# Two column tiles of 64 in place of four of 32 for the projections behind the product with V

## The chip, the cores and the metric

The kernel runs on one core of a Trainium2 chip. The metric is device time in microseconds (us). A core has five engines with queues of their own: TensorE (PE, with its weight loads listed apart as PEld), VectorE (DVE), ScalarE (ACT), GpSimd (POOL) and SyncE (SP), which issues most DMAs here.

## The reference

Two independent problems A and B are computed and their outputs laid side by side. Each is an attention block with 32 heads of 32 channels, 2048 positions, 1024 channels and a window of 256 keys:

```
qkv = (x @ wqkv) -> q, k, v          # x: 2048 x 1024, wqkv: 1024 x 3072
scores = q @ k.T * 32 ** -0.5        # kept where 0 <= query - key < 256
o = softmax(scores) @ v              # by head
out = o @ wo                         # wo: 1024 x 1024
```

All inputs and outputs are bfloat16.

## The kernel before

Four heads make a group (4 x 32 = 128 partitions), so there are 16 groups over both problems. TensorE has three kinds of work, and each uses the 128 x 128 array in a form of its own:

- The scores (line 537) multiply 32 rows (the channels of one head) by 64 columns (keys). Four heads and two halves of the keys lie in the array at the same time. The form is written 32*64 in the trace.
- The product with V and the row sums of the softmax (line 618) use all 128 rows (keys) and 32 columns (the channels of one head), four heads side by side: 128*32. This is `pv`, and there are 128 of them, one for each group and pair of query blocks.
- The projections (q and k, V, and the output) use all 128 rows. They all go through the helper `by_columns`. While `whole[0]` is true it issues one multiplication of 128 columns (line 193, 128*128). Otherwise it issues the same work as four multiplications of 32 columns each, at the column positions 0, 32, 64 and 96 (line 197, 128*32). Each multiplication has a weight load of its own.

The program is written out by a planner in steps; 152 of them hold scores. A step issues the scores (`session`), then those products with V that are due, then as much projection work as the planner has put there, in chains of eight multiplications over the 1024 input channels. Two ScalarE instructions per step take the exponential (line 547). Products are due in every second step, and `whole[0]` is set to false in exactly these:

```
        whole[0] = not (due and due[0][0] <= now)
        session(now)
        while due and due[0][0] <= now:
            ...
            pv(pg, pk)
```

So TensorE goes through scores, products and projections of 32 columns in a step with products, and through scores and projections of 128 columns in one without. After the last product of all, `whole[0]` is true again, and the rest of the output projection is issued whole.

The planner counts one projection multiplication of 512 elements at `NS_MM` = 216 ns in either form (`clock.pe += NS_MM`), so the form has no part in the order. The result of a chain is copied out of PSUM by ScalarE or VectorE (`evacuate`), whichever the planner's clock finds earlier.

Of the kernel before, what the change touches and what calls it, by code (L numbers as in the profile page):

```python
# [18 lines left out]
P = 128  # L19
# [64 lines left out]
def _fast_path(ctx, tc, cfg, problems, outs, consts, certify, osbp, ps_acc, ps_proj, last_stores):  # L84
    nc = tc.nc
# [105 lines left out]
    def by_columns(out, lo, hi, lhsT, rhs, start, stop):  # L191
        if whole[0]:
            nc.tensor.matmul(out[:, lo:hi], lhsT=lhsT, rhs=rhs, start=start, stop=stop,  # L193
                             skip_group_check=True)
            return
        for c in range(0, P, 32):
            nc.tensor.matmul(out[c:c + 32, lo:hi], lhsT=lhsT[:, c:c + 32], rhs=rhs, start=start,  # L197
                             stop=stop, tile_position=(0, c), skip_group_check=True)

    side = []  # L200
# [23 lines left out]
    def qk_steps(g, which, k, lo=0, hi=512, st_=None, last=True):  # L224
        pi = g // T
        st_ = {} if st_ is None else st_
        steps = []
        for ct in range(CT):
            def f(ct=ct):
                if "pp" not in st_:  # L230
                    st_["pp"] = new_pp()
                by_columns(st_["pp"], lo, hi, wqk[g][:, ct, which, :], xT[(pi, k)][:, ct, lo:hi],
                           ct == 0, ct == CT - 1)
                clock.pe += NS_MM * (hi - lo) / 512.0
                if ct == CT - 1 and last:
                    dst = qk_tiles(g)[which][:, k * 512:(k + 1) * 512]
                    evacuate(dst, st_["pp"][:])
                    clock.ready[(g, which, k)] = clock.banks[-1]
            steps.append((NS_MM * (hi - lo) / 512.0, f))
        return steps  # L240

    def v_steps(m, b):
        pi = m // (T // VG)
        k, a = divmod(b, QB)
        st_ = {}
        steps = []
        w_ = VG * P
        for h in range(512 // w_):
            for ct in range(CT):
                def f(ct=ct, h=h):  # L250
                    if "pp" not in st_:
                        st_["pp"] = new_pp()
                        if (m, k) not in vts:
                            vts[(m, k)] = vp.tile([P, QB, w_], BF16, name="vt")
                    by_columns(st_["pp"], h * w_, (h + 1) * w_,
                               xT[(pi, k)][:, ct, (a + h) * P:(a + h + 1) * P],
                               wv[m][:, ct, :], ct == 0, ct == CT - 1)
                    clock.pe += NS_MM * w_ / 512.0
                    if ct == CT - 1 and h == 512 // w_ - 1:
                        evacuate(vts[(m, k)][:, a:a + h + 1, :],  # L260
                                 st_["pp"][:].rearrange("p (h w) -> p h w", w=w_))
                steps.append((NS_MM * w_ / 512.0, f))
        return steps
# [12 lines left out]
    def last_steps(pi, b, ch):  # L276
        k, a = divmod(b, QB)
        st_ = {}
        steps = []
        for lo in (0, 256):  # L280
            for ct in range(CT):
                def f(ct=ct, lo=lo):
                    if ct == 0:
                        st_["pp"] = ps_acc.tile([P, 512], F32, name="acc")
                    by_columns(st_["pp"], lo, lo + 256, oTs[(pi, k)][:, ct, a * P:(a + 1) * P],
                               wo_sb[(pi, ch)][:, ct, lo:lo + 256], ct == 0, ct == CT - 1)
                    clock.pe += NS_MM / 2
                    if ct == CT - 1:
                        store(pi, b, ch, lo, lo + 256, st_["pp"])
                steps.append((NS_MM / 2, f))  # L290
        return steps
# [684 lines left out]
```

## Time and profile before

| what | value |
|---|---|
| median of 3 runs | 598.64 us (598.45 to 598.72) |
| the profiled execution, its own time | 598.88 us |
| its span, from first to last instruction | 597.2 us |
| TensorE busy | 590.3 us (99%) |
| ScalarE busy | 405.6 us (68%) |
| GpSimd busy | 365.2 us (61%) |
| VectorE busy | 349.7 us (59%) |
| mean granted TensorE clock | 1.000 of full speed |

A multiplication is pipelined: the next one starts while the last is still running, and their ends are modelled. What a multiplication costs TensorE is therefore the distance from its start to the next start, not the mean duration in a row. The four multiplications of 32 columns of one group start within about 10 ns of each other and run side by side. In a merged row of the timeline, the start is that of the first instruction, and the length runs to the end of the last.

### The profile page before, as it was taken

The numbers are of one execution on the slowest core, as the hardware profiler recorded it, in microseconds if no ns is written. First come the engines' busy times: TensorE is split into PE (matmuls) and PEld (weight loads), VectorE is DVE, ScalarE is ACT, GpSimd is POOL, SyncE is SP. The second block draws the span as 40 slices with busy tenths as digits, with TensorE's granted clock in tenths as the row PEclk, the third lists the DMA queues.
The fourth block names the chain that finished last, engine by engine and source line by source line (L and its number), as shares of the span: only waits on it lengthen the run. The fifth ranks groups of instructions, "written<-read, shape, count | busy, mean of one in ns | idle before, by whom it ended". The sixth has DMA issues, their size and how long they took to land. (4 is left out here: it accounts for less than half of the span.)

```text
span 597.2 us, 31193 instructions
## 1 busy us (share of the span) xinstructions
PE 590.3 (99%) x13863; PEld 358.9 (60%) x13863; DVE 349.7 (59%) x969; ACT 405.6 (68%) x506; POOL 365.2 (61%) x918
## 2 busy tenths in 40 slices
PE   9999999999999999999999999999999999999997
PEld 6666666666656756566656657755556665555443
DVE  1265676567667677774566656665566557576100
ACT  4667777877787787766566766676768777774332
POOL 0558667877768787766466666666666667665000
PEclk9999999999999999999999999999999999999999
DMA  9915110111026102645111100113020040114222
GB/s 241 183 38 145 39 40 3 40 40 37 4 48 100 39 4 57 107 94 115 33 39 39 27 14 4 41 37 87 7 74 21 3 109 13 56 56 132 66 80 75
DMA packets 86813, 35.63 MB, mean 60 GB/s; under 512 B 65552, under 2 KB 86160, under 8 KB 86672
## 3 DMA queue, kind: packets, MB, share of 16 engines
q1 hardware_dynamic: 85344, 33.18, 23.1%
q8 instruction: 110, 1.80, 1.3%
q10 hardware_dynamic: 1328, 0.39, 0.3%
q14 instruction: 31, 0.25, 0.2%
HBM read 17.83 MB, written 8.39 MB: 44 GB/s over the span
## 5 line engine op out<-in xcount | busy, mean ns | idle before, releaser
L547 ACT ACTIVATE pt<-st 128x1024 bf16<-128x1024 f32 x304 | 300.0, 1025 | 74.5 <-PE st L537 35.9
L558 POOL TENSOR_SCALAR_AFFINE_SELECT diag<-pt 128x256 bf16<-128x256 bf16 x512 | 215.6, 446 | 181.9 <-ACT pt L547 175.8
L571 POOL TENSOR_SCALAR_AFFINE_SELECT pt<-pt 128x512 bf16<-128x512 bf16 (+1 forms) x256 | 155.4, 626 | 0.0
L585 DVE TENSOR_TENSOR both<-diag,pt 128x512 bf16<-128x512 bf16 (+1 forms) x256 | 124.3, 525 | 15.9 <-POOL diag L558 11.7
L197 PE MATMUL pp<-xT,wqk 128*32 128x512 bf16 x2120 | 125.1, 379 | 0.0
L193 PE MATMUL pp<-xT,wqk 128*128 128x512 bf16 (+1 forms) x542 | 121.5, 361 | 0.0
L193 PE MATMUL pp<-wv,xT 128*128 128x256 bf16 x920 | 109.3, 273 | 0.0
L628 DVE STREAM_TRANSPOSE turned<-acc 128x128 f32<-128x128 f32 x128 | 39.8, 311 | 106.2 <-PE acc L618 106.2
L193 PEld LDWEIGHTS <-xT 128*128 128x128 bf16 x920 | 89.2, 98 | 19.6
L197 PEld LDWEIGHTS <-wqk 128*32 128x32 bf16 x2120 | 54.0, 97 | 44.7
L193 PE MATMUL pp<-wo_sb,oT 128*128 128x512 bf16 x347 | 78.3, 379 | 0.2 <-DVE unsafe_i L917 0.2
L537 PEld LDWEIGHTS <-kT 32*64 32x64 bf16 x3904 | 41.0, 103 | 58.5 <-issue 58.5
L193 PEld LDWEIGHTS <-wqk 128*128 128x128 bf16 x542 | 46.5, 98 | 45.1 <-DMA wqk<-in_A_wqkv_dram 0.2
L537 PE MATMUL st<-qT,kT 32*64 32x64 bf16 (+4 forms) x3904 | 65.7, 236 | 0.8 <-issue 0.8
L635 DVE STREAM_TRANSPOSE wide<-inv 128x256 f32<-128x256 f32 x128 | 56.9, 445 | 4.2
L193 PEld LDWEIGHTS <-oT 128*128 128x128 bf16 x363 | 34.3, 98 | 38.4 <-issue 0.2
L216 ACT CAST osb<-pp 128x512 bf16<-128x512 f32 x48 | 28.1, 586 | 42.8 <-PE pp L193 29.3
L636 DVE TENSOR_TENSOR oT<-acc,wide 128x256 bf16<-128x256 f32 x128 | 54.3, 424 | 4.4
L618 PE MATMUL acc<-pt,vt 128*32 128x128 bf16 (+2 forms) x1792 | 48.8, 223 | 0.0
L618 PEld LDWEIGHTS <-vt 128*32 128x32 bf16 x2816 | 43.5, 97 | 7.7 <-issue 0.4
L216 ACT CAST vt<-pp 128x512 bf16<-128x512 f32 x45 | 26.5, 588 | 31.7 <-PE pp L193 27.4
L216 ACT CAST kT<-pp 128x512 bf16<-128x512 f32 x55 | 32.2, 585 | 17.5 <-PE pp L197 14.3
(49 smaller groups left out, 378.0 us busy)
## 6 DMA issues: line engine op xcount, KB each, us to landing
out_dram<-osb SPq DMA_DIRECT2D x63, 128.0 KB, 1.9
wqk<-in_B_wqkv_dram SPq DMA_DIRECT2D x32, 128.0 KB, 3.3
wqk<-in_A_wqkv_dram SPq DMA_DIRECT2D x24, 128.0 KB, 3.0
wo_sb<-in_A_wo_dram SPq DMA_DIRECT2D x16, 128.0 KB, 2.4
wv<-in_B_wqkv_dram SPq DMA_DIRECT2D x16, 128.0 KB, 3.0
wo_sb<-in_B_wo_dram SPq DMA_DIRECT2D x16, 128.0 KB, 2.3
oT<-in_A_x_dram SPq DMA_DIRECT2D x4, 256.0 KB, 5.1
wv<-in_A_wqkv_dram SPq DMA_DIRECT2D x2, 512.0 KB, 6.2
```

The lines of the kernel that those rows point to most:

```text
L193: nc.tensor.matmul(out[:, lo:hi], lhsT=lhsT, rhs=rhs, start=start, stop=stop, skip_group_check=True)
L197: nc.tensor.matmul(out[c:c + 32, lo:hi], lhsT=lhsT[:, c:c + 32], rhs=rhs, start=start, stop=stop, tile_position=(0, c), skip_group_check=True)
L216: nc.scalar.copy(out=out, in_=in_)
L537: nc.tensor.matmul(scores[c * HALF:(c + 1) * HALF, r, a * HALF:(a + w_) * HALF], lhsT=kT[rows, keys], rhs=qT[rows, q:q + w_ * HALF], start ...
L547: nc.scalar.activation(out=pt[:, lo:lo + 2, :n * HALF], in_=scores[:, lo:lo + 2, :n * HALF], func=ACT.Exp, bias=-SHIFT, scale=cfg.scale)
L558: nc.gpsimd.affine_select(out=diags[(g, p)][:, :, h, lo:lo + HALF], in_=pt[:, :, a * HALF:(a + 1) * HALF], pattern=[[0, 4], [1, HALF]], co ...
L571: nc.gpsimd.affine_select(out=blk, in_=blk, pattern=[[0, 4], [-1, w_ * HALF]], compare_op=ALU.is_gt, fill=0.0, base=-HALF * (us[a][2] - 3) ...
L585: nc.vector.tensor_tensor(out=both[:, :, h, o:o + w_], in0=dg[:, :, h, o:o + w_], in1=pts[t][:, :, a:a + w_], op=ALU.add)
L618: nc.tensor.matmul(acc[32 * r:32 * r + 32, o:o + w_], lhsT=lhsT, rhs=src[:, r, :], start=(x == 0), stop=(x == len(moves) - 1), tile_positi ...
L628: nc.vector.transpose(out=turned[:], in_=acc[:, 2 * P:3 * P])
L635: nc.vector.transpose(out=wide[:], in_=inv[:].unsqueeze(3).to_broadcast([P, 2, QB, 32]))
L636: nc.vector.tensor_tensor(out=oTs[(pi, k)][:, t, (p % 2) * 256:(p % 2 + 1) * 256], in0=acc[:, 0:256], in1=wide[:], op=ALU.mult)
```

## The change

The loop in `by_columns` steps over the 128 columns by 64, so the work that was four multiplications of 32 columns becomes two of 64 columns, at the column positions 0 and 64, with two weight loads in place of four. Which chains are issued in this form and when stays as it was.

```
-        for c in range(0, P, 32):
-            nc.tensor.matmul(out[c:c + 32, lo:hi], lhsT=lhsT[:, c:c + 32], rhs=rhs, start=start,
+        for c in range(0, P, 64):
+            nc.tensor.matmul(out[c:c + 64, lo:hi], lhsT=lhsT[:, c:c + 64], rhs=rhs, start=start,
                              stop=stop, tile_position=(0, c), skip_group_check=True)
```

The instructions of TensorE at the first of these stretches, before, at its beginning (the last row sum with `ones`, then the first projection) and at its end (the last projection, then the first scores of the next step); the size behind a multiplication is its output, columns of the array by elements:

```order
L618 LDWEIGHTS ones_58
L618 MATMUL acc_605<-both_512,ones_58 32x128
L197 LDWEIGHTS wqk_123
L197 MATMUL pp_657<-xT_137,wqk_123 32x512
...
L197 LDWEIGHTS wqk_134
L197 MATMUL pp_697<-xT_122,wqk_134 32x512
L537 LDWEIGHTS kT_254
L537 MATMUL st_296<-qT_253,kT_254 64x256
```

The same two places of TensorE's order in the changed kernel:

```order
L618 LDWEIGHTS ones_58
L618 MATMUL acc_605<-both_512,ones_58 32x128
L197 LDWEIGHTS wqk_123
L197 MATMUL pp_657<-xT_137,wqk_123 64x512
...
L197 LDWEIGHTS wqk_134
L197 MATMUL pp_681<-xT_122,wqk_134 64x512
L537 LDWEIGHTS kT_254
L537 MATMUL st_296<-qT_253,kT_254 64x256
```

Before, the array's form was the same (128 rows, 32 columns) on both sides of the beginning; now the columns go from 32 to 64 there. At the end the rows go from 128 to 32 in both kernels, and the columns from 32 to 64 before, from 64 to 64 now. Between the two places the 64 multiplications before are 32 now. Nothing else moves on any engine: over the whole executed order, line 197 follows line 618 at 76 places, line 537 follows line 197 at 74, and line 618 follows line 197 at 2.

## Rows read from the trace of the kernel before

**Rows 1.** The page: busy time of TensorE; its granted clock in 40 slices.
```profile
PE 590.3 (99%) x13863; PEld 358.9 (60%) x13863; DVE 349.7 (59%) x969; ACT 405.6 (68%) x506; POOL 365.2 (61%) x918
...
PEclk9999999999999999999999999999999999999999
```

**Rows 2.** Waits of TensorE: waiting engine and line <- releaser: total us, times, longest.
```profile
PE pp L676 <- DVE ones L895: 1.3, 1, 1.3
PE pp L197 <- issue: 1.0, 1, 1.0
PE st L537 <- issue: 0.8, 1, 0.8
PE pp L193 <- DVE unsafe_i L917: 0.2, 1, 0.2
```

**Rows 3.** Longest waits of all engines, same columns.
```profile
POOL diag L558 <- ACT pt L547: 175.8, 130, 14.4
DVE turned L628 <- PE acc L618: 106.2, 66, 4.0
```

**Rows 4.** Groups by line and shape: xcount | busy us, mean ns | idle before.
```profile
L197 PE MATMUL pp<-xT,wqk 128*32 128x512 bf16 x2120 | 125.1, 379 | 0.0
L618 PE MATMUL acc<-both,ones 128*32 128x128 bf16 x896 | 31.9, 219 | 0.0
L197 PE MATMUL pp<-wo_sb,oT 128*32 128x512 bf16 x628 | 37.0, 379 | 0.0
L197 PE MATMUL pp<-wv,xT 128*32 128x256 bf16 x416 | 12.9, 273 | 1.0 <-issue 1.0
L197 PEld LDWEIGHTS <-wqk 128*32 128x32 bf16 x2120 | 54.0, 97 | 44.7
L537 PEld LDWEIGHTS <-kT 32*64 32x64 bf16 x3904 | 41.0, 103 | 58.5 <-issue 58.5
```

**Rows 5.** Timeline of TensorE, two steps: start us, length us, what, xcount.
```profile
131.99 0.28 PE L618 MATMUL acc<-both,ones 128*32 128x128 bf16 x8
132.10 2.33 PE L197 MATMUL pp<-xT,wqk 128*32 128x512 bf16 x40
134.37 0.42 PE L537 MATMUL st<-qT,kT 32*64 32x128 bf16 x24
134.72 1.47 PE L193 MATMUL pp<-xT,wqk 128*128 128x512 bf16 x6
136.03 1.91 PE L193 MATMUL pp<-wv,xT 128*128 128x256 bf16 x16
137.87 0.42 PE L537 MATMUL st<-qT,kT 32*64 32x256 bf16 x20
```

**Rows 6.** Timeline of TensorE at 134.36 us: last projection group, first scores.
```profile
134.04 0.39 PE L197 MATMUL pp<-xT,wqk 128*32 128x512 bf16 x4
134.37 0.24 PE L537 MATMUL st<-qT,kT 32*64 32x128 bf16 x2
```

**Rows 7.** Timeline of TensorE at 137.86 us: last whole projection, first scores.
```profile
137.66 0.27 PE L193 MATMUL pp<-wv,xT 128*128 128x256 bf16 x1
137.87 0.34 PE L537 MATMUL st<-qT,kT 32*64 32x256 bf16 x8
```

**Rows 8.** Timeline of TensorE, 554.8 to 555.7 us: last product, then whole projections.
```profile
554.84 0.28 PE L618 MATMUL acc<-both,ones 128*32 128x128 bf16 x8
555.05 0.82 PE L193 MATMUL pp<-wo_sb,oT 128*128 128x512 bf16 x3
```

**Rows 9.** Timeline of TensorE at 546.3 us: whole projections, then a product.
```profile
545.83 0.59 PE L193 MATMUL pp<-wo_sb,oT 128*128 128x512 bf16 x2
546.35 0.24 PE L618 MATMUL acc<-pt,vt 128*32 128x64 bf16 x7
```

**Rows 10.** Timeline of TensorE at 550.4 us: projections of 32 columns, then a product.
```profile
549.95 0.60 PE L197 MATMUL pp<-wo_sb,oT 128*32 128x512 bf16 x8
550.38 0.23 PE L618 MATMUL acc<-pt,vt 128*32 128x128 bf16 x4
```

**Rows 11.** Timeline of TensorE: the first and the last of 76 passages from products to projections.
```profile
30.10 0.29 PE L618 MATMUL acc<-both,ones 128*32 128x128 bf16 x8
30.21 0.39 PE L197 MATMUL pp<-xT,wqk 128*32 128x512 bf16 x4
...
550.83 0.28 PE L618 MATMUL acc<-both,ones 128*32 128x128 bf16 x8
550.94 0.39 PE L197 MATMUL pp<-wo_sb,oT 128*32 128x512 bf16 x4
```

## The prediction, made before the changed kernel ran

> **What bounds the kernel now.** I read the page first, then the waits, then the timeline of TensorE. On the page the reader is to see that TensorE is busy for 590.3 of 597.2 us and that the granted clock stands at full speed in all 40 slices [rows 1], so that no change of clock is in play. Busy time alone doesn't prove a bound, since multiplications overlap; the waits do. All of TensorE's waits come to 3.3 us, of which only 0.2 us lies after the start-up and is for another engine; two holes of 1.0 and 0.8 us have no releaser at all [rows 2]. The others wait for TensorE or for what follows it: VectorE alone waits 106.2 us for the products with V [rows 3]. So what TensorE loses or gains is lost or gained in the end, nearly one for one, and the question is how far apart its multiplications start.
>
> **Inside a run of projections nothing is to be had.** The stretch from 132.10 us holds 40 multiplications of 32 columns, ten groups of four [rows 5]. A group of four is 0.39 us long [rows 6], so the ten groups start (2.33 - 0.39) / 9 = 0.216 us apart. The whole form at 134.72 us has six in 1.47 us, one of which lasts 0.38: (1.47 - 0.38) / 5 = 0.218 us. Four narrow multiplications thus already run side by side at the pace of one whole one, and halving their number (2120 + 628 + 416 = 3164 become 1582 [rows 4]) takes away no time of the array. The same holds for the weight loads: they stand at 97 ns for 32 columns and 103 ns for 64 columns in the scores [rows 4], under a pace of 216 ns (and of 0.109 us for the V chains, from sixteen in 1.91 us with 0.27 for the last [rows 5 and 7]). I take the pace as unchanged. Below, it can't fall, as the array takes the same elements; above, the nearest row is 6 ns more for a wider load, which on all 3164 / 4 = 791 groups would be 4.7 us if none of it were hidden. The pace of 216 with four loads of 97 listed for each group shows that loads are hidden, so I take zero.
>
> **What the change puts in: a change of the array's form.** Now I compare passages between kinds of work, by the distance of starts.
> - Products to projections with the form kept (128 rows, 32 columns): the last two groups of row sums start at 131.99 and the projections at 132.10, 0.11 us for two groups, that is 0.055 each [rows 5]. The first and the last of the 76 such passages read the same, 30.10 to 30.21 and 550.83 to 550.94 [rows 11]. Nothing stands between the kinds.
> - Products to projections with the columns changed from 32 to 128 and the rows kept at 128: there is one, behind the last product. The same two groups start at 554.84 and the projections at 555.05, 0.21 us [rows 8]. It is 0.10 more than without a change.
> - The other way, 128 to 32 columns at 128 rows: the second whole projection starts at 545.83 + 0.59 - 0.38 = 546.04, the product at 546.35 [rows 9]: 0.31 against a pace of 0.216, so 0.09 to 0.10 more. With the form kept, 549.95 + 0.22 = 550.17 to 550.38 is the pace itself, 0.21 [rows 10].
> - Projections to scores, where rows and columns change: 134.04 to 134.37 from narrow ones, 0.33 against 0.216, so 0.11 [rows 6]; 137.66 to 137.87 from whole ones, 0.21 against 0.109, so 0.10 [rows 7].
>
> So any change of form costs about 0.10 us, whichever way it goes, no other engine is waited for in it, and a passage without a change costs nothing. The change makes one where there was none: from products of 32 columns to projections of 64. The trace has no row of 64 columns at 128 rows. From below it could cost nothing (if 32 to 64 is no change to the array); from above, 0.11 us plus one weight load of 0.10 standing open, 0.21. The nearest row is rows 8, with the same neighbour ahead and the same rows of the array; I take 0.105, between its 0.10 and rows 6's 0.11.
>
> The Trainium skill, "TensorEngine Tiling (Array Packing)", section "Key Properties", speaks against the change in the same sense: changing the tiling mode, as opposed to the tile, makes TensorE drain. Rows 8 to 10 agree with it, 0.10 us where the column size changes and nothing where it stays. By that rule 32 to 64 columns is a change of mode like any other.
>
> **Sum.** For each of the 76 passages from products to projections, of which the first and the last are shown [rows 11]:
> - the change of form, +0.105 us;
> - the first multiplication behind a change delays its successor a little: three whole ones take 0.82 us, 2 x 0.216 + 0.38 = 0.81 without that, and the six of rows 5 take 1.47 where 5 x 0.216 + 0.38 is 1.46 [rows 5 and 8]. So +0.01;
> - four narrow ones start over 0.39 - 0.38 = 0.01 us [rows 6]; two need an estimated third of it, so the last starts some 0.007 us earlier at the end of the run. So -0.007.
>
> That is 0.108 x 76 = 8.2 us. Twice, near the end, a product follows projections directly, now with a change from 64 to 32: 2 x (0.10 + 0.01) = 0.2 us [rows 9 and 10]. The 74 passages from projections to scores stay a change of form, at the price they have. Nothing hides the added time, since TensorE waits for no one after its start, and the other engines, which come later by it, already wait. Sum +8.4 us. The span goes from 597.2 to 605.6, the execution's own 598.88 to 607.3; that execution was 0.24 us above the median of 598.64, so the median goes to **607.0 us**, slower by 1.4%.
>
> **Rivals.**
> - *The array sees no change between 32 and 64 columns.* Then only the -0.007 x 76 = -0.5 us stays: 598.1, no change. For it: no row shows just this pair. Against it: rows 8 and 9 change the columns alone and pay in full. 6%.
> - *The way back gets free, the way in is paid.* Scores are 32 rows by 64 columns, so behind 64 columns only the rows change. If rows alone cost nothing, 74 x (0.10 + 0.01) = 8.1 us go, and 598.64 + 8.4 - 8.1 = 598.9. No row has a change of rows alone, so nothing excludes it; but the price in rows 6 and 7 is the same from 32 columns as from 128, which looks like one fixed charge and not like a charge by columns. 4%.
> - *Faster: the free way back decides.* The same free passage to the scores at 74 places, 8.1 us, with an entry that costs less than the measured changes. It wins by more than a measurement can tell once the entry is under (8.1 - 0.2 - 1.2) / 76 + 0.007 = 0.095 us in all, against 0.105 + 0.01 taken above; with a free entry the time is 598.6 - 0.5 - 8.1 = 590.0. It needs the column size to be what is charged on the way back and not on the way in, against rows 8. 3%.
> - *Slower still: the wide weight loads stand open.* If one load of 0.10 us [rows 4] is uncovered at each of the 76 entries, 7.6 us come on top: 614.6. Against it: passages into whole multiplications, with 128 columns to load, cost no more than those into 32 [rows 8 and 9]. 3%. The Trainium skill has a sentence on its side: "TensorEngine Tiling (Array Packing)", section "Restrictions", says that column tiling turns off the fast weight load, and "TensorE: Matmul & The Clock Gate", section "LDWEIGHTS (loading the stationary operand)", puts a load at its columns / 1.2 ns, an estimated 53 ns for 64 columns. With two such in a row open at each entry it would be about the same 614.8 by that rule; no row here has such a load at 128 rows.
>
> **How the numbers follow.** The forecast has 84%, the rivals 6, 4, 3 and 3. The forecast's own spread: an entry of 0.085 to 0.13 in all in place of 0.108 gives 605.2 to 608.7; I widen this a little to **605.0 to 608.8**, which leaves out the four rivals (16%) and a few per cent of the forecast itself. A change under 0.2%, 1.2 us, can't be told from none here. Slower holds the forecast and the last rival, 87%; no change the first two, 10%; faster 3%.
>
> **What would show it.** Line 197 with 1060, 314 and 208 multiplications of 64 columns; two groups of row sums to the first projection at 0.21 us in place of 0.11; ten groups still in about 2.33 us; the passages from projections to scores still at 0.32 and 0.21 us; TensorE's waits as small as before; the span 8.4 us longer, spread evenly over the steps with products. A passage into 64 columns at 0.11 us, or one to the scores without its 0.10, or a pace of groups other than 0.216, would make the forecast wrong at that term.

## The result and the profile after

| | before | after |
|---|---|---|
| median | 598.68 us (598.45 to 599.45) | 606.25 us (606.01 to 606.45) |
| span of the profiled execution | 597.2 us | 604.7 us |

The changed kernel is slower by 7.6 us; the ratio is 1.0127, with a 95% interval of 1.0116 to 1.0139. The forecast was 607.0 us, within 605.0 to 608.8.

The page of the changed kernel, TensorE's busy time and granted clock:

```profile
PE 587.5 (97%) x12202; PEld 364.1 (60%) x12281; DVE 349.0 (58%) x969; ACT 405.7 (67%) x506; POOL 365.0 (60%) x918
...
PEclk9999999999999999999999999999999999999999
```

The clock is full throughout, as in [rows 1]. The first thing to see is a trap: there are 12281 weight loads and 12202 multiplications, where before the two counts were equal. 79 multiplications left no record. TensorE's waits show the same thing:

```profile
PE pp L193 <- issue: 9.5, 60, 0.2
PE pp L676 <- DVE ones L895: 1.3, 1, 1.3
PE turned L689 <- DMA oT<-in_A_x_dram: 0.8, 2, 0.6
PE pp L193 <- PE st L537: 0.6, 4, 0.2
PE pp L193 <- DVE unsafe_i L917: 0.2, 1, 0.2
```

The 9.5 us in the first row look like the loss, being larger than it, but they are 60 places, 0.16 us idle each, at which the first whole projection behind the scores left no record; the fourth row has four more of them. Line 193 has 418 multiplications for q and k here where it had 478 before, and 328 for the output where it had 347, while their weight loads, 542 and 363, are the same in both: 60 and 19 records are missing, the 79. (An unchanged kernel below has the same row.) What is gone against [rows 2] are the two idle times of 1.0 and 0.8 us without a releaser, called holes from here on. Line 197 by shape, then the shortest, median and longest of its multiplications (ns) with the first and last start (us):

```profile
L197 PE MATMUL pp<-xT,wqk 128*64 128x512 bf16 x1060 | 126.1, 382 | 0.0
L197 PEld LDWEIGHTS <-wqk 128*64 128x64 bf16 x1060 | 55.3, 109 | 48.0
L197 PE MATMUL pp<-wo_sb,oT 128*64 128x512 bf16 x314 | 37.2, 381 | 0.0
L197 PE MATMUL pp<-wv,xT 128*64 128x256 bf16 x208 | 12.9, 274 | 0.0
```

```profile
L197 PE MATMUL pp<-xT,wqk x1060: 379/379/403, 30.4 to 539.7; 128*64 128x512 bf16 x177
L197 PE MATMUL pp<-wv,xT x208: 272/273/297, 200.0 to 404.7; 128*64 128x256 bf16 x104
```

The counts are half those of [rows 4], as written. The median is unchanged; the longest is 24 ns over it, and these are the first ones behind the products. The ends of multiplications are modelled, so this longer one counts only as far as starts show it too, below. Now the same two steps as in [rows 5], about 2 us later, on TensorE's timeline (start us, length us, what, count):

```profile
133.91 0.28 PE L618 MATMUL acc<-both,ones 128*32 128x128 bf16 x8
134.13 2.35 PE L197 MATMUL pp<-xT,wqk 128*64 128x512 bf16 x20
136.41 0.42 PE L537 MATMUL st<-qT,kT 32*64 32x128 bf16 x20
```

The last two groups of row sums start at 133.91 and the projections at 134.13, 0.22 us, where they took 0.11. The ten groups take 2.35 in place of 2.33. One longer first multiplication (0.024) explains that: (2.35 - 0.38 - 0.02) / 9 = 0.217 us is the old pace. The way out of such a stretch, to the scores, and the passage to a product near the end:

```profile
135.88 0.60 PE L197 MATMUL pp<-xT,wqk 128*64 128x512 bf16 x4
136.41 0.25 PE L537 MATMUL st<-qT,kT 32*64 32x128 bf16 x4
```

```profile
561.03 0.60 PE L197 MATMUL pp<-wo_sb,oT 128*64 128x512 bf16 x4
561.56 0.24 PE L618 MATMUL acc<-pt,vt 128*32 128x128 bf16 x4
```

The last group starts one pace behind the first of the row, at 135.88 + 0.216 = 136.10, and the scores 0.31 us later: the change of form, 0.10, is still paid, although only the rows of the array change now (128 to 32, with 64 columns on both sides). Against 0.33 in [rows 6] it is a little shorter, since two starts spread less than four. The passage to the product pays 561.56 - 561.25 = 0.31 where [rows 10] had the pace of 0.21.

### The profile page after: what moved, and what is told of

Its sections match the earlier page's. It is cut to its first block, busy times and chain, and to the rows that moved or that the text cites. A ratio compares the mean times of both kernels' runs of the same rounds, so it can differ in the third digit from the quotient of the medians.

```text
span 604.7 us, 27950 instructions
## 1 busy us (share of the span) xinstructions
PE 587.5 (97%) x12202; PEld 364.1 (60%) x12281; DVE 349.0 (58%) x969; ACT 405.7 (67%) x506; POOL 365.0 (60%) x918
## 5 line engine op out<-in xcount | busy, mean ns | idle before, releaser
L197 PE MATMUL pp<-xT,wqk 128*64 128x512 bf16 x1060 | 126.1, 382 | 0.0
L193 PE MATMUL pp<-xT,wqk 128*128 128x512 bf16 (+1 forms) x482 | 108.4, 358 | 7.5 <-issue 7.0
L197 PEld LDWEIGHTS <-wqk 128*64 128x64 bf16 x1060 | 55.3, 109 | 48.0
L193 PE MATMUL pp<-wo_sb,oT 128*128 128x512 bf16 x328 | 75.1, 379 | 2.6 <-issue 2.1
```

Of the source, the lines that this page charges most:

```text
L197: nc.tensor.matmul(out[c:c + 64, lo:hi], lhsT=lhsT[:, c:c + 64], rhs=rhs, start=start, stop=stop, tile_position=(0, c), skip_group_check=True)
```

## The experiments

**The kernel before, unchanged (`again`)**, for its two holes.

> The kernel before, unchanged, for its two holes in TensorE's work without a releaser (1.0 and 0.8 us), which the changed kernel's trace doesn't have. If they come from how TensorE gets its instructions, they are there again at about 246 and 285 us. If they belong to one execution, they are elsewhere or missing. Time 598.7 either way, within 0.3%.

It measured 599.47 us, ratio 1.0008 (0.9997 to 1.0019). The first fence is the kernel before, the second this run of the same program; `<-issue` is idle time for which the profile shows no releaser:

```profile
246.12 0.42 PE L537 MATMUL st<-qT,kT 32*64 32x192 bf16 x18
247.29 0.29 PE L537 MATMUL st<-qT,kT 32*64 32x256 bf16 x2 [0.75 <-issue]
247.52 0.82 PE L193 MATMUL pp<-wo_sb,oT 128*128 128x512 bf16 x3
...
283.29 1.70 PE L197 MATMUL pp<-wv,xT 128*32 128x256 bf16 x56
286.03 0.73 PE L197 MATMUL pp<-wv,xT 128*32 128x256 bf16 x20 [1.03 <-issue]
```

```profile
246.06 0.42 PE L537 MATMUL st<-qT,kT 32*64 32x192 bf16 x18
246.83 0.30 PE L537 MATMUL st<-qT,kT 32*64 32x256 bf16 x2 [0.35 <-issue]
...
283.27 1.26 PE L197 MATMUL pp<-wv,xT 128*32 128x256 bf16 x40
285.39 1.38 PE L197 MATMUL pp<-wv,xT 128*32 128x256 bf16 x44 [0.85 <-issue]
```

They come in the same rows of like instructions, though not at the same instruction of a row, so they belong to the program. (This trace has a third, of 0.3 us by starts, at 542 us.) Both lie in or behind V chains, the projection chains for V, in narrow form, where TensorE gets eight instructions (four loads, four multiplications) in 0.109 us. Counted by starts the second one costs 1.2 us: the last group ahead of it starts at 283.29 + 1.70 - 0.27 = 284.72, the next was due at 284.83 and came at 286.03. The first costs 1.0: from the first scores to the whole projections behind them it is 247.52 - 246.12 = 1.40 us, where `thin2` below takes 0.36. Together 2.2 us.

What ends them can be read from the trace. A DMA queue of kind "instruction" moves packets of 16 KB, and the pages of the kernel before, of the changed kernel and of `all32` below list it so (packets, MB, share of 16 engines):

```profile
q8 instruction: 110, 1.80, 1.3%
q8 instruction: 98, 1.61, 1.1%
q8 instruction: 153, 2.51, 1.7%
```

Its bytes go with TensorE's instructions: `all32` has 2 x 5475 = 10950 more than the kernel before and moves 0.71 MB more, an estimated 65 bytes for each. The hole at 284.72 ends 1.29 us behind the landing of such a packet, at 284.74; the one at 246.27 ends 1.73 us behind one. So it is in every trace that has holes: all 51 that cost over 0.15 us by starts, 36 of them in `all32`, end 1.2 to 1.7 us behind the landing of a packet, though such times are only 11 to 14% of the execution. In these holes TensorE waits for its own instructions. Why a packet comes late is not shown.

**All projections in one multiplication of 128 columns (`wide128`).**

```
-        if whole[0]:
+        if True:
             nc.tensor.matmul(out[:, lo:hi], lhsT=lhsT, rhs=rhs, start=start, stop=stop,
...
```

> All projections as one multiplication of 128 columns, also behind the products. Theory (each change of the array's form costs 0.10 us): 77 passages from products pay 0.106 + 0.010 less 0.010 for the spread of four narrow starts, and two more from projections to products, together +8.4 us: 607.1, or 605.3 if the two holes go. The first multiplication behind the change lasts 10 ns longer, not 24 as with 64 columns. Rival (multiplications of 64 columns are slow in themselves, by their loads): no pair of 64 is left, so 598.7.

It measured 605.38 us, ratio 1.0106 (1.0089 to 1.0123): the value of the theory with the holes gone. That pairs of 64 columns are slow in themselves is out as the cause, as there are none. Its line 193, shortest, median and longest in ns:

```profile
L193 PE MATMUL pp<-wv,xT x1024: 272/273/284, 11.3 to 495.1; 128*128 128x256 bf16 x171
L193 PE MATMUL pp<-wo_sb,oT x478: 376/379/391, 248.9 to 597.7; 128*128 128x512 bf16 x160
```

The longest are 11 to 12 ns over the median, not 24; 106 multiplications left no record here, many of them such first ones. That is some 0.013 us less at each of 76 passages, 1.0 us; the two kernels differ by 0.87, which fits, but the intervals of their ratios overlap.

**64 columns in every second step with products (`half`).**

The edit against the changed kernel, cut (`cols` starts as `[32]`):

```
-        for c in range(0, P, 64):
+        n = cols[0]
+        for c in range(0, P, n):
...
         whole[0] = not (due and due[0][0] <= now)
+        if not whole[0]:
+            cols[0] = 96 - cols[0]
```

> 64 columns in every second step with products only, 32 in the others. Theory: 37 passages at 0.104 + 0.024 - 0.007 = 0.121 us, +4.5 us: 603.2 with the two holes, 601.4 without. Both rivals (slow pairs, or a cost of leaving the product) give half of the 7.6 us too, 602.5; the run is to show that the cost adds up by places and none is hidden.

It measured 604.18 us, ratio 1.0092 (1.0075 to 1.0109), span 602.2. That is above what was expected by 1.0 us. All 37 passages carry the change of form, but holes came elsewhere, the largest in a stretch of 32 columns:

```profile
81.04 1.25 PE L198 MATMUL pp<-xT,wqk 128*32 128x512 bf16 x20
83.05 0.61 PE L198 MATMUL pp<-xT,wqk 128*32 128x512 bf16 x8 [0.76 <-issue]
```

By starts there are four, together 1.9 us. With 37 x 0.121 = 4.5 us and 0.3 us less of holes than before, 4.2 of the 5.0 us in the span are accounted for. Of the rest 0.4 us passes behind the last multiplication, which starts at 598.1 of 602.2 us, before at 593.5 of 597.2; 0.4 stays open.

**The change of form moved one multiplication later (`late64`).**

The edit against the changed kernel, cut (`fresh[0]` is set to true by each product):

```
-        for c in range(0, P, 64):
...
+        n = 32 if fresh[0] else 64
+        fresh[0] = False
+        for c in range(0, P, n):
...
+        fresh[0] = True
```

> The first projection multiplication behind the products in four of 32, all others of the stretch in two of 64, so that the change of form is moved one multiplication later. Theory (the change of form is paid wherever it stands): the passage from products to projections is at 0.11 us for two groups again, and the step from 32 to 64 costs 0.104 + 0.024: +9.3 us, 608.0 with the two holes, 606.2 without. Rival (the cost belongs to leaving the product, its last results and signals): 598.7 or little more.

It measured 606.36 us, ratio 1.0125 (1.0108 to 1.0142), as the changed kernel. Its timeline at the first such stretch, in two windows:

```profile
30.11 0.29 PE L622 MATMUL acc<-both,ones 128*32 128x128 bf16 x8
30.22 0.39 PE L199 MATMUL pp<-xT,wqk 128*32 128x512 bf16 x4
...
30.54 0.62 PE L199 MATMUL pp<-xT,wqk 128*64 128x512 bf16 x4
```

From the product to the projections it is 0.11 us again; the group of four is followed after 0.32 in place of 0.216. Leaving the product has no price. The change of form has, wherever it stands.

**32 and 64 columns in turn (`alternate`).**

The edit against the changed kernel, cut (the first line stands in `by_columns`, the last in each product):

```
-        for c in range(0, P, 64):
...
+        n = cols[0] = 96 - cols[0]
+        for c in range(0, P, n):
...
+        cols[0] = 64
```

> The projections behind the products take 32 and 64 columns in turn, multiplication by multiplication, beginning with 32: 379 changes from 32 to 64 and 336 back inside the stretches. Theory: 379 x (0.104 + 0.024) + 336 x (0.096 + 0.010) = 84 us more: about 683 (681 without the two holes). Rival (pairs of 64 are slow in themselves): half as many pairs as in the changed kernel, 602.5.

It measured 681.68 us, ratio 1.1377 (1.1352 to 1.1401), against 681 expected without the holes, and its trace has none. With the 2.2 us of the holes added back, 82.6 + 2.2 = 84.8 us for 717 changes (the 715, and two in front of a product) are 0.118 us each. Its multiplications by shape (mean ns behind the busy time):

```profile
L198 PE MATMUL pp<-xT,wqk 128*32 128x512 bf16 x1112 | 110.6, 387 | 0.0
L198 PE MATMUL pp<-xT,wqk 128*64 128x512 bf16 x504 | 102.4, 403 | 0.0
```

Here nearly every multiplication is the first behind a change: with 64 columns it lasts 403 ns in place of 379, with 32 columns 387 in the mean. The time bears this out: 379 x (0.104 + 0.024) + 338 x (0.096 + 0.010) is 84.3 us, while 0.010 for either load would give 79.0.

**64 columns everywhere (`all64`) and 32 columns everywhere (`all32`).** The test for the whole form is `if False:` in the changed kernel and in the kernel before.

> All projections in two of 64 columns, also behind the scores. Theory: as the changed kernel, but 78 more passages into a load of 64 columns, 0.014 us more each than into 128 columns, and 0.003 of spread at their ends: +1.3 us, and some changes among the first transposes, to 0.7 us: 607.6 to 608.3. Rival (pairs of 64 are slow in themselves): more than double the pairs, so about 598.7 + 2.5 x 7.6 = 618.

> All projections in four of 32 columns, also behind the scores: no form is new, 5500 more multiplications and as many loads. Theory: 78 ends of stretches with 0.011 us of spread, and some changes among the first transposes: +0.9 to 1.6 us, 599.6 to 600.3. If the holes come from how TensorE gets its instructions, there are many more of them, and the time is some us higher still; if not, two or none.

The first measured 610.25 us, ratio 1.0184 (1.0167 to 1.0202), 2 us above what was expected. Holes are that: by starts there are three, together 2.0 us, the largest in a V chain of 64 columns at the start:

```profile
13.60 0.41 PE L197 MATMUL pp<-wv,xT 128*64 128x256 bf16 x3
15.27 1.80 PE L197 MATMUL pp<-wv,xT 128*64 128x256 bf16 x29 [1.26 <-issue]
```

Pairs slow in themselves would have made it 618. The second measured 634.2 us, ratio 1.0577 (1.0538 to 1.0616), though no form is new in it. Its page and its waits:

```profile
PE 604.7 (96%) x19338; PEld 383.7 (61%) x19338; DVE 347.6 (55%) x969; ACT 406.0 (64%) x506; POOL 363.7 (57%) x918
...
PEclk9989999999999999999999999999999999999999
```

```profile
PE pp L197 <- issue: 10.8, 12, 3.3
PE acc L618 <- issue: 7.7, 12, 1.8
PE st L537 <- issue: 1.3, 4, 0.5
```

With 19338 multiplications in place of 13863, the idle time without a releaser is 19.8 us in place of 1.8, at all three kinds of work. No records are missing here (as many loads as multiplications), so these are true holes; by starts those over 0.15 us come to 26 us. They grow with the number of TensorE's instructions, by far more than I expected. A smaller part of the loss is the clock, which is at 9 in all 40 slices of every other page. Two stretches by engine, with the granted clock behind them:

```profile
14.50:17.80 3.30, 3.30 (x104) 3.30 (x96) 0.00 (x0) 1.17 (x2) 0.00 (x0) 0.50 1.70 205
31.60:34.80 3.20, 3.20 (x44) 1.26 (x40) 0.00 (x0) 1.94 (x2) 1.06 (x3) 0.50 0.02 5
```

The clock fell to the lower of its two levels, 1.2 GHz, shortly behind the two largest holes, of 3.3 and 2.2 us idle, and stood there for 3.4 us each time; at half speed that is an estimated 3.4 us lost in all. Of the 35.1 us the holes make some 24 (26 less the 2.2 of before) and the clock 3.4; 0.9 to 1.6 were expected without either, 1.2 pass behind the last multiplication, and some 5 us stay open.

**The kernel before with 128 columns in two steps (`thin2`).**

```
-        if whole[0]:
+        if whole[0] or step[0] in (70, 80):
...
+        step[0] = now
```

> The kernel before, with 128 columns in just the two steps with products (the 71st and the 81st) behind which TensorE has its holes at 246 and 285 us; there the V chains of 256 elements stand in four of 32. 150 multiplications and as many loads fewer, two more changes of form. Theory (the holes are where TensorE's instructions don't come fast enough): both go, 2.1 us, against 2 x (0.106 + 0.010 - 0.011) = 0.2 us for the changes: about 596.9, 0.3% faster. Rival (the shortage only moves to the next dense stretch): 598.8 to 599.0.

It measured 597.92 us against 599.33 of the kernel before beside it, ratio 0.9977 (0.9966 to 0.9988): faster by 1.4 us, with 0.7 to 2.0 as the interval, which holds the 1.9 expected. The two places, and a third:

```profile
246.74 0.42 PE L538 MATMUL st<-qT,kT 32*64 32x192 bf16 x20
247.10 0.61 PE L193 MATMUL pp<-wo_sb,oT 128*128 128x512 bf16 x2
...
283.32 2.89 PE L193 MATMUL pp<-wv,xT 128*128 128x256 bf16 x25
...
406.08 0.39 PE L538 MATMUL st<-qT,kT 32*64 32x64 bf16 x26
406.93 0.25 PE L538 MATMUL st<-qT,kT 32*64 32x64 bf16 x10 [0.46 <-issue]
```

The twenty scores at 246 and the V chain at 283 run through. Three smaller holes have come, of 0.6, 0.2 and 0.2 us by starts, the largest at 406, so about half of the 2.2 us moved. The profiled execution is one of the slower ones, 598.98 us with a span of 597.3, no shorter than before: the 1.0 us gained between its first scores and its last multiplication goes again ahead of the one and behind the other. So the gain rests on the medians. This version is faster than both kernels, at the price of two changes of form.

## Why the prediction came out

The direction, the mechanism and the time were right. By its own steps:

- **TensorE is the bound, nothing absorbs the loss.** Held: the span grew by 7.5 us and the median by 7.6, and the only new wait, 0.8 us for an input among the first transposes, makes the first scores about 0.1 us later.
- **No gain within a run.** Held for the array: the pace is 0.217 with two, 0.216 with four. Not held for what feeds it, see the last point.
- **A change of form costs 0.105 us.** Held: 0.22 less 0.11 at the first projection, and about 0.10 at every passage shown, for columns alone, for rows alone (0.31 less 0.21, which the trace of before could not show), and for both. `late64` and `alternate` show that it is the change, wherever it stands.
- **The first multiplication behind a change, +0.01 us.** Mis-sized: 0.024. I had taken it from whole multiplications. With 64 columns it is more than twice that; `alternate` shows it in time, and `wide128` against the changed kernel fits it. The trace of before had such a load behind a change, in the scores: the 0.24 us of [rows 6] is longer than the 0.219 that a multiplication of the same 128 elements takes in [rows 4]. I had read that row for its start only. The rule of the Trainium skill cited with the last rival, "TensorEngine Tiling (Array Packing)", section "Restrictions", that column tiling turns off the fast weight load, would fit the 109 ns that a load of 64 columns lasts here, where one of 128 columns lasts 98; which loads are fast ones no run shows. (The estimate beside that rival, two loads of 53 ns open at 76 entries, comes to 615.1, not 614.8.)
- **The spread, -0.007 us, and the two passages back, 0.2 us.** Held, as far as two decimals show: 0.31 for 0.33 to the scores, 0.31 for 0.21 to the product.
- **The holes.** Not in the sum. I saw them in [rows 2] and took them as given. They are 2.2 us, and they went with half of the instructions of line 197.

So 76 x (0.104 + 0.024 - 0.007) + 0.2 = 9.4 us, less 2.2, is 7.2. The last multiplications, before and after (ns, then first and last start):

```profile
L193 PE MATMUL acc<-wo_sb,oT x16: 272/272/273, 591.8 to 593.5; 128*128 128x256 bf16 x16
L193 PE MATMUL acc<-wo_sb,oT x16: 272/273/273, 599.0 to 600.7; 128*128 128x256 bf16 x16
```

They come 7.2 us later, and the other 0.3 of the 7.5 us in the span passes behind them. The predicted 8.4 was near because two errors, +1.1 and -2.2, go against each other. That is luck: with the holes gone and the load as I had it, the time would have been 604.8, just outside the range.

Of the rivals, a free change between 32 and 64 columns is excluded by 0.22 us at the passage; the free way back, and with it the faster case, by the 0.31 us to the scores; and wide loads standing open at full length by the 0.024 us that are open.

That the holes are a shortage of instructions is shown by four things: they return in the same rows, vanish where the stretch ahead is thinned, multiply with the count, and end 1.2 to 1.7 us behind the landing of an instruction packet. What makes some packets late, and so which dense stretch is hit, stays open.

## What to carry to other kernels

Where TensorE is the bound, count the places at which neighbouring multiplications change the rows or columns of the array that they use, and read the price from one such place by the distance of starts; here it is 0.10 us plus 0.01 to 0.024 for the first load. A narrower form that matches its neighbour can be worth more than half as many instructions. And look at idle time of TensorE that nothing releases: if it follows dense narrow instructions and ends behind a packet of the instruction queue, thinning that one stretch can pay, even with a change of form; here it paid 0.2%.

## What was not expected of the hardware

A change of the rows alone, with 64 columns on both sides, costs the same 0.10 us as any other. And four instructions where one would do are free only as long as they are few: 5475 multiplications more, with as many loads, cost 35 us in `all32`, 19.8 of them as idle time in 28 holes, and an estimated 3.4 by the clock that fell behind the two largest.
